# A spectral filter feeding a soft mixture of experts: bank pairs taken in turn, the fold in its own tiles, signs on ScalarE

## The chip, the cores and the metric

The kernel runs on one core of one Trainium2 chip. The core has five engines with instruction queues of their own: TensorE (PE in the profile; its weight loads are listed as PEld), VectorE (DVE), ScalarE (ACT), GpSimd (POOL) and SyncE (SP), which here issues nearly all transfers. Sixteen DMA engines carry the transfers between HBM and the on-chip memory SBUF. TensorE writes its results to PSUM, which has eight banks of 2 KB per partition. The metric is the device time of one execution in microseconds; a time of a kernel is the median of its runs.

## What is computed

```
x: (8, 2496, 256)   filt_r, filt_i: (1249, 256)   phi: (256, 32)   w1: (8, 256, 1024)   w2: (8, 1024, 256)

X = rfft(x, axis=1);  Y = X * (filt_r + i filt_i);  y = irfft(Y, n=2496, axis=1)     # global filter
x = y.reshape(19968, 256)
logits = x @ phi                                    # 32 slots, 4 for each of 8 experts
d = softmax of logits over the 19968 tokens
slot_input = d.T @ x
slot_out[e] = relu(slot_input[e] @ w1[e]) @ w2[e]   # for each expert e
c = softmax of logits over the 32 slots
out = c @ slot_out
```

Everything is float32. The transform of length 2496 is split as 39 x 64. It is a real transform, so half of the spectrum is enough.

## The kernel before

**Stages.** The forward transform of a batch has two stages. The first (length 39, over six units of a batch, `PIECE`, L53) starts from data that is *folded*: sums and differences of mirrored tokens. `load_x` (L345) brings a unit's tokens into a tile xt, `fold_x` (L358) makes the sums and differences in four elementwise operations, `s1_unit` (L380) does four pairs of matmuls into two PSUM banks, and ScalarE copies the result to a tile called at (L407). `store_a` (L413) writes it to a scratch tensor in HBM, a_dram, and `load_ash` (L438) reads it back with the other index ahead. `x_pair` (L474) is the second stage (length 64): eight matmuls into two PSUM banks, then on VectorE the complex product with the filter, which is two multiplications (L510, L512) and two sums (L513, L514). For batches 6 and 7 the sums run on GpSimd and the second multiplication writes to SBUF. `t_pair` (L516) turns the result, ScalarE copies it, and `l_unit` (L531) multiplies by phi, still in the frequency domain. From the logits of a group of batches a long chain of small steps (`chain`, L576) makes the softmax over tokens and adds to the slots' inputs; it is cut into pieces at its `yield`s, and `hop` puts a piece or two into each slot. Batch 0 takes another way into its first stage (`first_stage`, `turn`) that needs no fold and no trip through HBM. After the last batch come the experts and the output (from L1071).

**Slots.** The main loop (L937) runs over slots n = 0 to 81, ten to a batch. Each even slot below 80 has one x_pair, so 40 pairs in all; t_pair follows one pair later, l_unit in the odd slot behind it. `slot_of` (L81) gives each of the 42 first-stage units of batches 1 to 7 its slot: batch 1's units lie in slots 0 to 4, one in each, later batches have six units in ten slots, one in each even slot and one more in an odd one. Slot 64 (`last_s1`) has the last. From there x has the only bank pair of its own, and the other one goes to the chain.

**What sets the order.** Each engine works its queue in order. The program text is not the order by itself: a planner places each engine's instructions by priorities and by its own estimate of when inputs are ready. `behind` (L330) chains instructions of one queue strictly, `not_before` (L354) says that an instruction may not be placed ahead of another one; it is a lower bound, with no wait on the chip. All transfers of L337 on SP are chained in the order of the program text. TensorE's order within a pair is given by such bounds through `held`: x (even slot), the first-stage unit of that slot, t of the pair before, then in the odd slot l and the other unit. The fold's operations have bounds only for the first two units.

**Tiles and banks around the change.** PSUM's eight banks: two for x (`ps_x`), two for the first stage (`ps_s1`), two for t and l (`ps_t`), two for the chain (`ps_c`). So x of one pair needs the banks that VectorE still reads for the pair before. Of xt there are `XB` = 6 tiles, of at `AB` = 4, and one (`EB` = 1) for the fold's intermediate sums and differences, called eo. The fold's first two operations read xt and write eo, the last two read eo and write back into xt. So an xt tile comes free when the unit's matmuls are done. The second of the four operations runs on VectorE (`FD = (1,)`), the others on GpSimd; the first two units (`early`) run on VectorE alone. Six loads are issued ahead of the loop, and each `store_a` of a unit issues one more (`next_x`). `sign_tables` (L812) multiplies the imaginary filter table of each of ten columns by a sign, the first two on VectorE, eight on GpSimd.

Of the kernel before, what the change touches and what calls it, by code (L numbers as in the profile page):

```python
# [40 lines left out]
P = 128  # L41
# [4 lines left out]

CPB = NT // 2
PPB = CPB // 2
XB = 6
EB = 1  # L50
FD = (1,)
AB = 4
PIECE = ((0, 1), (1, 3), (3, 5), (5, 7), (7, 9), (9, 11))  # L53
NU = len(PIECE)
NK = N2 // 4
# [227 lines left out]
def fft_soft_moe(ctx, tc, x0, w0, x, ff, phi, wx, cst, w1q, out):  # L283
# [65 lines left out]
        xts[b, c] = t  # L349

    eos = {}
    held = [None] * 6

    def not_before(ins, other):  # L354
# [3 lines left out]
    def fold_x(b, u):  # L358

        lo, hi = PIECE[u]  # L360
        w = (hi - lo) * P
        xs = xts.pop((b, u)).rearrange("q k a d -> q (k a d)")[:, 0 : 4 * w].rearrange("q (k a d) -> q k a d", k=2, a=2)
        eo = proda.tile([P, 2, 2, DIM], F32, tag="eo", name=f"eo{b}_{u}", bufs=EB)
        sd = eo.rearrange("q f a d -> q (f a d)")[:, 0 : 4 * w].rearrange("q (f a d) -> q f a d", f=2, a=2)
        early = (b, u) < (1, 2)
        for k, (o, i0, i1, op) in enumerate((
            (sd[:, 0], xs[:, 0], xs[:, 1], ALU.add),
            (sd[:, 1], xs[:, 0], xs[:, 1], ALU.subtract),
            (xs[:, 0], sd[:, :, 0], sd[:, :, 1], ALU.add),
            (xs[:, 1], sd[:, ::-1, 0], sd[:, ::-1, 1], ALU.subtract),  # L370
        )):
            eng = dve if early or k in FD else pool_e
            ins = eng.tensor_tensor(out=o, in0=i0, in1=i1, op=op)  # L373
            if early:
                not_before(ins, held[4])
        eos[b, u] = xs

    a_dram = {}

    def s1_unit(b, u, floor=None):  # L380
        if u == 0:
            a_dram[b] = scr.tile([P, NT, DIM], F32, tag="a_dram", name=f"a_dram{b}")
        lo, hi = PIECE[u]
        w = (hi - lo) * P
        eo = eos.pop((b, u))
        both = ps_s1[0].tile([P, 2, 2, DIM], F32, tag="s1", name=f"s1_{b}_{u}")
        bf = both.rearrange("q r f d -> q r (f d)")[:, :, 0 : 2 * w]
        with tc.high_priority():
            for c, r in ((1, 0), (1, 1), (0, 0), (0, 1)):
                q = slice(64 * r, 64 * r + 64)  # L390
                ins = pe.matmul(  # L391
                    bf[64 * c : 64 * c + 64, r],
                    w1q_t[q, c],
                    eo[q, c].rearrange("q f d -> q (f d)"),
                    start=True,
                    stop=True,
                )
                held[1] = ins
                if floor is None:
                    behind("pe", ins)  # L400
                else:
                    not_before(ins, floor)
                    if held[2] is not None:
                        not_before(ins, held[2])
        at = proda.tile([P, 4 * DIM], F32, tag="at", name=f"at{b}_{u}", bufs=AB)
        av = at[:, 0 : 4 * w].rearrange("q (f r d) -> q f r d", f=2, r=2)
        copied[0] = act.copy(av, bf.rearrange("q r (f d) -> q f r d", f=2))  # L407
        stores.append((b, u, at))
# [4 lines left out]
    def store_a():  # L413

        while stores:
            b, u, at = stores.pop(0)
            ad = a_dram[b].rearrange("(f r c m) t d -> f r c m t d", f=2, r=2, c=2)
            for c in range(2):
                if u:
                    m = PK * (u - 1)  # L420
                    dst = a_dram[b].rearrange("(g c m) t d -> c g m t d", g=4, c=2)[c, :, m : m + PK]
                    issue(
                        dst.rearrange("g m t d -> (m t) g d"),
                        at[64 * c : 64 * c + PK * HR].rearrange("q (g d) -> q g d", g=4),
                    )
                    continue
                for r in range(2):
                    dst = ad[:, r, c, NJ] if r else ad[c, r, :, NJ]
                    p0 = 64 * c + HR * r
                    issue(dst.rearrange("f t d -> t f d"), at[p0 : p0 + HR, 0 : 2 * DIM].rearrange("q (f d) -> q f d", f=2))  # L430
            next_x()

    ys = {}
    lts = {}
# [39 lines left out]
    def x_pair(b, i):  # L474

        ash = ashs.pop((b, i)).rearrange("q (c k) d -> q c k d", k=2)
        ps = ps_x.tile([P, 2, 2, DIM], F32, tag="x", name=f"x_{b}_{i}")
        first = []
        for r, k in ((0, 0), (0, 1), (1, 0), (1, 1)):
            for lo, hi in ((0, 1), (1, 2)) if i + k == 0 else ((0, 2),):  # L480
# [30 lines left out]
        add, part = (pool_e, y) if b >= PA else (dve, ps)  # L511
        dve.tensor_tensor(out=part, in0=ps, in1=frv, op=ALU.mult)  # L512
        add.tensor_tensor(out=y[:, 1], in0=part[:, 1], in1=t2[:, 1], op=ALU.add)  # L513
        add.tensor_tensor(out=y[:, 0], in0=part[:, 0], in1=t2[:, 0], op=ALU.subtract)  # L514

    def t_pair(b, i):  # L516

# [294 lines left out]
    def sign_tables(c):  # L812
        if c < CPB:
            fi = ff_t[:, c, 1]
            eng = dve if c < 2 else pool_e
            eng.tensor_scalar(out=fi, in0=fi, scalar1=C("sgn", c, c + 1), scalar2=None, op0=ALU.mult)

    NS = BATCH * CPB
    units = [(b, u) for b in range(1, BATCH) for u in range(NU)]
# [6 lines left out]
    def next_x():  # L826
        if xnext:
            load_x(*xnext.pop(0))

    def split_next(n):  # L830
        for b, u in at_slot.get(n, ()):
            fold_x(b, u)

    w0_t = ypool.tile([P, 1024], F32, tag="y", name="w0_t")
# [24 lines left out]
    def load_to(n):  # L859
        while loads:  # L860
            b, i = loads[0]
            if n < max(b * CPB + 2 * i - (3 if b < 2 else 2 * NA - 1), slot_of(b, NU - 1) + (2 if b < 3 else 3)):
                break
            load_ash(*loads.pop(0))

# [8 lines left out]
    s1_unit(1, 0)  # L874
    sign_tables(0)
    sign_tables(1)
    split_next(0)
    last = {bs[-1]: g for g, bs in enumerate(GROUPS)}
    active = []
    late_pool = []  # L880
# [56 lines left out]
    for n in range(NS + LT):  # L937
        if n < NS:
            load_to(n)
            if n == CPB // 2:  # L940
                issue(cst_t[:, NEAR:FAR], cst[:, NEAR:FAR])
            if n == NS - 2 * CPB:
                behind("sp", sp.dma_start(cst_t[:, FAR:], cst[:, FAR:]))
            split_next(n + 1)
            store_a()
        if n % 2 == 0 and n < NS:
            x_pair(*divmod(n // 2, PPB))
        if n < NS:
            sign_tables(n + 2)
            if n + 2 < CPB:  # L950
                turn(n + 2)
        if n % 2 == 0:
            for b, u in at_slot.get(n, ()):
                s1_unit(b, u, held[0])
        if n % 2 == 0 and n >= LT:
            t_pair(*divmod(n // 2 - 1, PPB))
        if n == last_s1:
            store_a()
            proda_cm.__exit__(None, None, None)
            ps_s1_cm.__exit__(None, None, None)  # L960
            ps_s1[0] = ctx.enter_context(tc.tile_pool(name="ps_s2", bufs=2, space=PSUM))
            late_cm, lp = open_pool("late", WL, "right")
            work2_cm, lp2 = open_pool("work2", 1, "left")
            late_pool.extend((lp, lp2))
            wl = iter(range(WL))
# [15 lines left out]
        floor[0] = (held[2] if n % 2 else held[5]) if n > last_s1 else None  # L981
        hop_slot(n)
        floor[0] = None
        if n % 2:
            for b, u in at_slot.get(n, ()):
                s1_unit(b, u, held[2] or held[0])
        if n == FREE:
            load_ws(ypool, "y", (YB - 3 * CPB + NS % YB - CPB) // 2, 2)
            big[0] = ypool.tile([P, PPB, 2, 2, DIM], F32, tag="yb", name="yb_last", bufs=1)
# [208 lines left out]
```

## Time and profile before

| | |
|---|---|
| median of 3 runs | 433.5 us (433.19 to 433.61) |
| the profiled execution | 434.7 us |
| its span, first to last instruction | 432.8 us |
| mean granted TensorE clock | 0.908 |
| TensorE matmul, VectorE, ScalarE, GpSimd busy | 82%, 63%, 40%, 48% of the span |
| SP's transfer queue | 71.4% of 16 DMA engines |

All times of the trace are microseconds from the span's start. An instruction's idle time is that of its engine just ahead of it, and the releaser named with it is what ended that idle time: "DVE eo L373 <- DMA xt<-in_x" means that VectorE stood still ahead of an instruction of line 373 that writes eo, until a transfer into xt had landed. In that notation `out<-in` names the tile written and the tiles read, with numbers left out. A busy TensorE is not one at its peak, since its matmuls overlap and their ends are modelled. The share of DMA is the mean over the 16 engines.

### The profile page before, as it was taken

What the parts mean: (1) busy time and instruction counts of PE and PEld (TensorE: products, weight loads), DVE (VectorE), ACT (ScalarE), POOL (GpSimd) and SP (SyncE); (2) the same over time, 40 slices, a digit from 0 to 9 for tenths busy, and PEclk for the clock granted to TensorE, in tenths of its full rate; (3) what the DMA queues carried; (4) which work ended last, traced back from release to release, by engine and by line L of the source; (5) the groups of instructions that cost most, each with busy time, mean ns of one, the idle gap of its engine ahead of it and who ended that gap; (6) DMA issues with size and microseconds to landing.
All of it is one profiled execution on the core that took longest, in us unless ns stands there. A gap on an engine that the chain in (4) does not pass through costs nothing.

```text
span 432.8 us, 10012 instructions
## 1 busy us (share of the span) xinstructions
PE 352.8 (82%) x4054; PEld 211.2 (49%) x4054; DVE 274.1 (63%) x423; ACT 172.5 (40%) x354; POOL 208.8 (48%) x200
## 2 busy tenths in 40 slices
PE   8959485786795869688779798998998999999970
PEld 7623132333442545344336454555655763687860
DVE  2761566666566958767677888467756645288640
ACT  3443133423335435243255344545423643186530
POOL 0499999686445745456664640444224130363000
PEclk9998799968999698998898899999999999999655
DMA  8995848786748564876776568676469579189997
GB/s 315 399 299 170 272 143 249 226 247 227 232 137 274 154 195 116 242 233 199 247 215 181 153 175 248 179 243 217 123 218 334 229 253 322 38 347 411 418 416 304
DMA packets 42013, 103.88 MB, mean 240 GB/s; under 512 B 4252, under 2 KB 22556, under 8 KB 39792
## 3 DMA queue, kind: packets, MB, share of 16 engines
q1 hardware_dynamic: 41278, 102.89, 71.4%
q8 instruction: 32, 0.52, 0.5%
q10 hardware_dynamic: 690, 0.36, 0.3%
q14 instruction: 13, 0.11, 0.1%
HBM read 63.11 MB, written 40.12 MB: 239 GB/s over the span
## 4 chain that ended last, share of the span: by engine, by line
PE 32%; DMA 20%; DVE 19%; POOL 12%; issue 5%; ACT 5%; SPq 2%; ACTq 0%; DVEq 0%; POOLq 0%
DMA xt<-in_x 14%; POOL xt L373 7%; PE x L485 5%; PE s L391 4%; DVE t L510 3%; DVE x L512 3%; PE out L1148 3%; DMA out<-ob 3%; POOL eo L373 3%; PE v L574 2%; ACT at L407 2%; SPq L337 2%; PE dd L574 2%; DMA phi_t<-in_phi 2%; PE s L574 2%
## 5 line engine op out<-in xcount | busy, mean ns | idle before, releaser
L373 POOL TENSOR_TENSOR xt<-eo 128x512 f32<-128x512 f32 (+1 forms) x80 | 93.6, 1191 | 11.1 <-DVE eo L373 3.2
L373 POOL TENSOR_TENSOR eo<-xt 128x512 f32<-128x512 f32 (+1 forms) x40 | 62.9, 1571 | 65.7 <-DMA xt<-in_x 64.4
L485 PE MATMUL x<-ash,cst_t 64*64 64x512 f32 (+3 forms) x352 | 58.7, 656 | 32.8 <-DVE y L514 18.2
L407 ACT COPY at<-s 128x1024 f32<-128x1024 f32 (+1 forms) x42 | 39.6, 942 | 108.4 <-PE s L391 97.6
L510 DVE TENSOR_TENSOR t<-x,ff_t 128x1024 f32<-128x1024 f32 x40 | 48.9, 1221 | 33.0 <-PE x L485 21.1
L373 DVE TENSOR_TENSOR eo<-xt 128x512 f32<-128x512 f32 (+1 forms) x44 | 29.0, 663 | 60.0 <-DMA xt<-in_x 38.5
L391 PE MATMUL s<-xt,w1q_t 64*64 64x512 f32 (+1 forms) x336 | 49.9, 666 | 5.0 <-POOL xt L373 5.0
L529 ACT COPY yt<-t 128x512 f32<-128x512 f32 x80 | 43.5, 594 | 17.6 <-PE t L523 17.4
L540 PE MATMUL l<-yt,phi_t 128*32 128x128 f32 x640 | 37.3, 286 | 9.1 <-ACT yt L529 7.3
L523 PEld LDWEIGHTS t<-cst_t,y 128*128 128x128 f32 x232 | 26.6, 147 | 25.4 <-issue 18.1
L485 PEld LDWEIGHTS x<-ash,cst_t 64*64 64x64 f32 (+1 forms) x352 | 14.3, 145 | 48.6 <-DVE y L514 21.9
L1148 PE MATMUL out<-so,st 32*128 32x256 f32 x468 | 35.5, 337 | 2.0 <-ACT ob L1153 1.0
L512 DVE TENSOR_TENSOR x<-x,ff_t 128x1024 f32<-128x1024 f32 x30 | 36.8, 1227 | 0.5
L513 POOL TENSOR_TENSOR y<-y,t 128x512 f32<-128x512 f32 x9 | 11.5, 1274 | 48.5 <-DVE y L512 44.4
L523 PE MATMUL t<-cst_t,y 128*128 128x128 f32 x232 | 34.5, 289 | 0.2
L1148 PEld LDWEIGHTS out<-so,st 32*128 32x128 f32 x468 | 30.9, 222 | 5.9 <-ACT ob L1153 3.1
L540 PEld LDWEIGHTS l<-yt,phi_t 128*32 128x32 f32 x640 | 19.2, 110 | 23.8 <-ACT yt L529 21.6
L1153 DVE COPY ob<-out 128x512 f32<-128x512 f32 (+1 forms) x40 | 25.0, 670 | 8.6 <-DMA out<-ob 5.5
L1153 ACT COPY ob<-out 128x512 f32<-128x512 f32 (+1 forms) x40 | 21.8, 581 | 14.9 <-PE out L1148 6.9
L391 PEld LDWEIGHTS s<-xt,w1q_t 64*64 64x64 f32 x336 | 14.5, 154 | 24.6 <-issue 16.3
L551 ACT COPY lt<-l 128x128 f32<-128x128 f32 x40 | 10.7, 269 | 33.1 <-PE l L540 33.1
L574 PE MATMUL s<-y,dd 128*32 128x256 f32 x232 | 18.4, 381 | 0.0
(124 smaller groups left out, 534.5 us busy)
## 6 DMA issues: line engine op xcount, KB each, us to landing
xt<-in_x SPq DMA_DIRECT2D x35, 512.0 KB
ash<-a_dram SPq DMA_DIRECT2D x35, 512.0 KB
out<-ob SPq DMA_DIRECT2D x17, 1024.0 KB
a_dram<-at SPq DMA_DIRECT2D x70, 240.0 KB
w<-in_wx SPq DMA_DIRECT2D x22, 512.0 KB
x_t<-in_x SPq DMA_DIRECT2D x5, 512.0 KB
ff_t<-in_ff SPq DMA_DIRECT2D x10, 256.0 KB
ff_t<-in_wx SPq DMA_DIRECT2D x5, 512.0 KB
```

Source lines behind the costliest of these rows:

```text
L373: ins = eng.tensor_tensor(out=o, in0=i0, in1=i1, op=op)
L391: ins = pe.matmul(bf[64 * c : 64 * c + 64, r], w1q_t[q, c], eo[q, c].rearrange("q f d -> q (f d)"), start=True, stop=True,)
L407: copied[0] = act.copy(av, bf.rearrange("q r (f d) -> q f r d", f=2))
L485: ins = pe.matmul(ps[64 * k : 64 * k + 64, r, lo:hi], w[rows], ash[rows, lo:hi, k], start=True, stop=True)
L510: dve.tensor_tensor(out=t2, in0=ps[:, ::-1], in1=fiv, op=ALU.mult)
L512: dve.tensor_tensor(out=part, in0=ps, in1=frv, op=ALU.mult)
L523: ins = pe.transpose(pt[:, dh, r, :], ys[b, 2 * i + c][:, r, dh * P : (dh + 1) * P], ident)
L529: act.copy(yt[:, c], pt)
L540: ins = pe.matmul(pl[32 * j : 32 * j + 32], phi_t[:, dh, :], yt[:, j // 2, dh, :, N2 * (j % 2) : N2 * (j % 2) + N2], start=(dh == 0), stop ...
L574: line(pe.matmul(*a, **k))
L1148: nc.tensor.matmul(prs[k][:, mm, :], sts[n][q, hs, c0 : c0 + P], so[q, ho], start=(i == 0), stop=(i == 2))
L1153: copy(ob[:, nm * k : nm * (k + 1), :], prs[k])
```

## The change

1. Second transform and first stage share two bank pairs. `x_pair` takes them in turn; `s1_unit` takes the pair that the latest x_pair did not take. When the first stage has ended (`proda_open`), x keeps to one pair as before.
2. The fold writes its sums and differences to a tile sd (`DB` = 2) and its result to a tile eo (`EB` = 2), no longer back into xt. There are five xt tiles instead of six and three at tiles instead of four. For batch 1 the first two operations both run on VectorE.
3. The fold is called three slots ahead of its unit instead of one, behind the slot's x_pair instead of ahead of it. Its VectorE operations may not be placed ahead of the latest pair's last sum (`added`).
4. The next load of xt is issued ahead of each fold instead of behind each store.
5. First-stage units come behind t_pair in even slots, and ahead of l_unit in odd ones, with the latest t or x as their bound.
6. The ash loads of batch 1 may come one slot sooner.
7. All ten signs are done by ScalarE, as a copy with a scale for each partition.

```diff
-XB = 6
-EB = 1
+XB = 5
+EB = 2
+DB = 2
 FD = (1,)
-AB = 4
+AB = 3
...
+    added = [None]
...
         xs = xts.pop((b, u)).rearrange("q k a d -> q (k a d)")[:, 0 : 4 * w].rearrange("q (k a d) -> q k a d", k=2, a=2)
-        eo = proda.tile([P, 2, 2, DIM], F32, tag="eo", name=f"eo{b}_{u}", bufs=EB)
-        sd = eo.rearrange("q f a d -> q (f a d)")[:, 0 : 4 * w].rearrange("q (f a d) -> q f a d", f=2, a=2)
+        sd = proda.tile([P, 4 * DIM], F32, tag="sd", name=f"sd{b}_{u}", bufs=DB)
+        eo = proda.tile([P, 4 * DIM], F32, tag="eo", name=f"eo{b}_{u}", bufs=EB)
+        sd, eo = (
+            t[:, 0 : 4 * w].rearrange("q (f a d) -> q f a d", f=2, a=2) for t in (sd, eo)
+        )
         early = (b, u) < (1, 2)
         for k, (o, i0, i1, op) in enumerate((
             (sd[:, 0], xs[:, 0], xs[:, 1], ALU.add),
             (sd[:, 1], xs[:, 0], xs[:, 1], ALU.subtract),
-            (xs[:, 0], sd[:, :, 0], sd[:, :, 1], ALU.add),
-            (xs[:, 1], sd[:, ::-1, 0], sd[:, ::-1, 1], ALU.subtract),
+            (eo[:, 0], sd[:, :, 0], sd[:, :, 1], ALU.add),
+            (eo[:, 1], sd[:, ::-1, 0], sd[:, ::-1, 1], ALU.subtract),
         )):
-            eng = dve if early or k in FD else pool_e
+            eng = dve if early or k in FD or (b == 1 and k < 2) else pool_e
             ins = eng.tensor_tensor(out=o, in0=i0, in1=i1, op=op)
             if early:
                 not_before(ins, held[4])
-        eos[b, u] = xs
+            elif eng is dve and added[0] is not None:
+                not_before(ins, added[0])
+        eos[b, u] = eo
...
+    turn_of = [1]
+
+    def pair_banks(k):
+        return (ps_s1[0], "s1") if k and proda_open[0] else (ps_x, "x")
+
+    proda_open = [True]
...
-        both = ps_s1[0].tile([P, 2, 2, DIM], F32, tag="s1", name=f"s1_{b}_{u}")
+        pool, tag = pair_banks(1 - turn_of[0])
+        both = pool.tile([P, 2, 2, DIM], F32, tag=tag, name=f"s1_{b}_{u}")
...
-            next_x()
...
-        ps = ps_x.tile([P, 2, 2, DIM], F32, tag="x", name=f"x_{b}_{i}")
+        turn_of[0] = 1 - turn_of[0]
+        pool, tag = pair_banks(turn_of[0])
+        ps = pool.tile([P, 2, 2, DIM], F32, tag=tag, name=f"x_{b}_{i}")
...
-        add.tensor_tensor(out=y[:, 0], in0=part[:, 0], in1=t2[:, 0], op=ALU.subtract)
+        added[0] = add.tensor_tensor(out=y[:, 0], in0=part[:, 0], in1=t2[:, 0], op=ALU.subtract)
...
-            eng = dve if c < 2 else pool_e
-            eng.tensor_scalar(out=fi, in0=fi, scalar1=C("sgn", c, c + 1), scalar2=None, op0=ALU.mult)
+            act.activation(fi, fi, AF.Copy, scale=C("sgn", c, c + 1))
...
         for b, u in at_slot.get(n, ()):
+            next_x()
             fold_x(b, u)
...
-            if n < max(b * CPB + 2 * i - (3 if b < 2 else 2 * NA - 1), slot_of(b, NU - 1) + (2 if b < 3 else 3)):
+            if n < max(b * CPB + 2 * i - (4 if b < 2 else 2 * NA - 1), slot_of(b, NU - 1) + (2 if b < 3 else 3)):
...
-    split_next(0)
+    for n in range(3):
+        split_next(n)
...
-            split_next(n + 1)
             store_a()
         if n % 2 == 0 and n < NS:
             x_pair(*divmod(n // 2, PPB))
         if n < NS:
+            split_next(n + 3)
             sign_tables(n + 2)
...
-        if n % 2 == 0:
-            for b, u in at_slot.get(n, ()):
-                s1_unit(b, u, held[0])
         if n % 2 == 0 and n >= LT:
             t_pair(*divmod(n // 2 - 1, PPB))
+        for b, u in at_slot.get(n, ()):
+            s1_unit(b, u, held[5])
         if n == last_s1:
             store_a()
             proda_cm.__exit__(None, None, None)
+            proda_open[0] = False
...
-        if n % 2:
-            for b, u in at_slot.get(n, ()):
-                s1_unit(b, u, held[2] or held[0])
```

## The prediction

> **What bounds the kernel now.** I read the totals first, then the span cut into four stretches, then the waits of the stretches that have the first stage in them, and last the instructions around one wait.
>
> ```profile
> span 432.8 us, 10012 instructions
> PE 352.8 (82%) x4054; PEld 211.2 (49%) x4054; DVE 274.1 (63%) x423; ACT 172.5 (40%) x354; POOL 208.8 (48%) x200
> ```
>
> No engine is full. The busy time by stretch (columns: busy us and instructions of each engine, granted clock, share of the 16 DMA engines, GB/s):
>
> ```profile
> core 0: us, PE busy (x) PEld busy (x) DVE busy (x) ACT busy (x) POOL busy (x), PEclk, DMA share, GB/s
> 18.00:80.00 62.00, 42.14 (x320) 18.68 (x319) 36.03 (x46) 21.65 (x36) 59.68 (x49) 0.92 0.73 231
> 80.00:262.00 182.00, 146.21 (x1600) 78.63 (x1600) 130.22 (x174) 70.41 (x133) 103.16 (x80) 0.89 0.69 206
> 262.00:331.00 69.00, 64.13 (x810) 37.88 (x810) 45.39 (x62) 29.50 (x61) 22.52 (x18) 1.00 0.66 214
> 331.00:433.00 102.00, 84.37 (x1211) 62.75 (x1211) 54.62 (x125) 43.75 (x107) 21.84 (x50) 0.86 0.79 303
> ```
>
> The change acts in the first two rows: before 18 us there is only loading and batch 0's start, after 262 nothing is folded any more. In the first, GpSimd is full (59.68 of 62). In the second, 182 us long, VectorE works 130.22 and stands 51.8. The waits of these two stretches (total us, times, longest), first 18 to 80, then 80 to 262:
>
> ```profile
> DVE eo L373 <- POOL xt L373: 20.6, 12, 3.7
> ```
> ```profile
> POOL eo L373 <- DMA xt<-in_x: 64.4, 21, 5.6
> DVE eo L373 <- DMA xt<-in_x: 38.5, 16, 5.4
> PE x L485 <- DVE yb L514: 12.0, 5, 3.2
> DVE t L510 <- PE x L485: 10.6, 9, 2.1
> PE x L485 <- DVE y L514: 9.6, 5, 3.6
> ```
>
> Of VectorE's 51.8 idle us, 38.5 stand ahead of one instruction, the second op of the fold (L373), and what it waits for is the load of xt. One such place:
>
> ```profile
> 78.86 0.71 SPq L337 DMA_DIRECT2D xt<-in_x  x1
> 81.79 1.23 DVE L510 TENSOR_TENSOR t<-x,ff_t 128x1024 f32<-128x1024 f32 x1 [1.21 <-PE x L485]
> 85.04 0.69 DVE L373 TENSOR_TENSOR eo<-xt 128x512 f32<-128x512 f32 x1 [2.02 <-DMA xt<-in_x]
> 85.65 1.23 DVE L512 TENSOR_TENSOR x<-x,ff_t 128x1024 f32<-128x1024 f32 x1
> 86.91 0.69 DVE L513 TENSOR_TENSOR yb<-x,t 128x512 f32<-128x512 f32 x1
> 87.51 0.68 DVE L514 TENSOR_TENSOR yb<-x,t 128x512 f32<-128x512 f32 x1
> 88.25 1.98 PE L485 MATMUL x<-ash,cst_t 64*64 64x512 f32 x8 [2.33 <-DVE yb L514]
> 90.56 1.99 PE L391 MATMUL s<-xt,w1q_t 64*64 64x512 f32 x8
> ```
>
> The fold has been put between the two multiplications of a pair. Its load was issued at 78.86 and is there 6 us later; meanwhile L512, whose input has long been ready, stands behind it, then the two sums, and then TensorE, because the one pair of PSUM banks for x is free only after the second sum (2.33 us). And the fold is not urgent at all: the load is issued when an xt buffer comes free, so the fold runs as soon as its data lands, with six buffers up to five units before the first stage wants it. A wait for a distant transfer has been queued ahead of near work.
>
> **The second transform in two bank pairs.** x of pair p+1 no longer waits for the sums of pair p, but for the ScalarE copy of the first stage that last used the other two banks; the first stage of pair p waits for the sums of pair p-1. Warm, the PE pieces of one pair are:
>
> ```profile
> 110.77 1.09 PE L485 MATMUL x<-ash,cst_t 64*64 64x512 f32 x8
> 111.68 1.04 PE L391 MATMUL s<-xt,w1q_t 64*64 64x512 f32 x8
> 112.65 1.09 PE L523 MATMUL t<-cst_t,y 128*128 128x128 f32 x8
> 114.75 0.72 PE L540 MATMUL l<-yt,phi_t 128*32 128x128 f32 x16
> ```
> ```profile
> L373 POOL TENSOR_TENSOR xt<-eo 128x512 f32<-128x512 f32 (+1 forms) x54 | 63.3, 1193 | 10.2 <-DVE eo L373 3.2 <-PE t L523 2.9 <-DVE al L748 2.4
> L373 POOL TENSOR_TENSOR eo<-xt 128x512 f32<-128x512 f32 (+1 forms) x26 | 40.6, 1562 | 64.8 <-DMA xt<-in_x 64.4
> L512 DVE TENSOR_TENSOR x<-x,ff_t 128x1024 f32<-128x1024 f32 x22 | 27.0, 1226 | 0.2
> L510 DVE TENSOR_TENSOR t<-x,ff_t 128x1024 f32<-128x1024 f32 x22 | 26.8, 1220 | 10.8 <-PE x L485 10.6
> L407 ACT COPY at<-s 128x1024 f32<-128x1024 f32 (+1 forms) x27 | 25.2, 934 | 68.8 <-PE s L391 65.7 <-DMA xt<-in_x 3.2
> L373 DVE TENSOR_TENSOR eo<-xt 128x512 f32<-128x512 f32 (+1 forms) x26 | 17.4, 668 | 39.2 <-DMA xt<-in_x 38.5 <-POOL xt L373 0.6
> ```
>
> These groups are of 80 to 262: 22 pairs and 27 first-stage units, so a pair takes 182/22 = 8.27 us, with 130.22/22 = 5.92 of VectorE work. The new loop goes from the sums of p-1 through t (1.09), s (1.04), the copy (0.93), x (1.09) and VectorE's four ops (1.22 + 1.23 + 0.69 + 0.68 = 3.82) to the sums of p+1: 7.97 us for two pairs, 4.0 for one. That lies below 5.92, so the banks themselves bind nothing; s standing after t costs nothing for the same reason. The waits of x for the sums (12.0 + 9.6) and of VectorE for x (10.6) can go.
>
> **The fold.** Three ops for GpSimd and one for VectorE stay, in tiles of their own; VectorE's op now comes behind the second sum of the pair before. An xt buffer is freed by the first two ops instead of by the first stage, and its next load is issued four units ahead: at 27/22 units per pair, more than three pairs, or 18 us at 5.92, against the 6 us that a load took. So the 38.5 us go. On SP the load has moved behind the store of the unit before and ahead of later stores and loads of ash. It waits for the fold of the unit before, which ends about 0.7 us behind the sums; the store ahead of it waits for t, s and the copy, 3 us behind them. So it holds nothing up. At the start three loads now stand ahead of batch 1's first store, behind the first folds; that store is wanted only by pair 5, for which the ash loads also come one slot sooner. What is late next if I am wrong on this: the ash load behind it, and x. After VectorE's op, GpSimd needs 2 x 1.19 us; the first stage comes one whole VectorE pair later, at least 3.82 us. With two sd and two eo tiles GpSimd's earlier op has its tile. Three at buffers instead of four: each has two further units, over 9 us, to be stored. I cost these at nothing; cover gone, each is in the fourth rival below.
>
> **GpSimd and the signs.** In the stretch 18 to 80 VectorE's fold waits 20.6 us for GpSimd, which has one tile for sums and differences and does the signs in between.
>
> ```profile
> L816 POOL TENSOR_SCALAR ff_t<-ff_t,cst_t 128x256 f32<-128x256 f32 x8 | 8.0, 1002 | 16.6 <-DMA ff_t<-in_ff 16.6
> L709 ACT COPY u<-u 128x240 f32<-128x240 f32 x12 | 3.8, 368 | 1.1 <-PE u L574 1.1
> ```
>
> GpSimd loses 8.0 us of signs and four first ops of batch 1 (4 x 1.56 = 6.2): 59.7 - 14.2 = 45.5. VectorE gains 4 x 0.67 = 2.7. ScalarE's ten signs have no row before; nearest is its copy of 128x240, 0.37 us, and the copy of a whole unit, 0.93, bounds it above; nothing of it is a gain on ScalarE, so 3.7 to 9.3 us on an engine with 62 - 21.65 = 40 idle. I take 0.4 each, at no cost to the end. The transfers' floor there is 0.73 x 62 = 45.3. The fullest that this trace keeps any engine over a long stretch is TensorE after 262: 64.13/69 = 0.93. So this stretch should take 45.5/0.93 = 49 us: **minus 13**. Bounds: 45 (minus 17), and 58 (minus 4) if only the signs and a quarter of the waits go.
>
> **The steady stretch.** Floors: VectorE 130.2; TensorE 146.21 x 0.89 = 130.1 at full clock; transfers 0.69 x 182 = 125.6; GpSimd 103.2. Three of them stand level, so what goes from VectorE's waits cannot go on for ever. Take away the 38.5 alone and leave the other 13.3 us of idle as they are, as a stand-in for new small waits: 143.5. Then there is a cost that the old order avoided. These rows show VectorE and GpSimd in each other's way, the same work with company (first and last row) and without:
>
> ```profile
> 143.49 3.69 DVE L680 TENSOR_TENSOR d<-lg,m_run 117x512 f32<-117x512 f32 x3
> 296.33 2.00 DVE L680 TENSOR_TENSOR d<-lg,m_run 117x512 f32<-117x512 f32 x3
> ```
> ```profile
> 120.09 1.27 POOL L373 TENSOR_TENSOR eo<-xt 128x512 f32<-128x512 f32 x1 [2.25 <-DMA xt<-in_x]
> 128.65 1.78 POOL L373 TENSOR_TENSOR eo<-xt 128x512 f32<-128x512 f32 x1 [4.05 <-DMA xt<-in_x]
> ```
>
> So far the load's landing released both engines together, and VectorE's 0.69 us op got in first. From now on it starts when the sums end, with GpSimd perhaps inside an op of 1.2 us. At a GpSimd share of 103.2/150 = 0.69 and half an op lost, 27 x 0.69 x 0.6 = 11 us; in a regular rhythm GpSimd would have finished (2.4 + 1.6 us of a pair's 5.9) when VectorE comes, so I take half, 6: **150 us, minus 32**. Bounds: 130.2/0.93 = 140 (minus 42), and 143.5 + 27 x 0.9 = 168 (minus 14), a wait of most of an op at each fold.
>
> The Trainium skill ("SBUF — State Buffer", Who interferes with whom) speaks against this edit here: a VectorE instruction with two SBUF inputs and a GpSimd instruction that reads SBUF share one port pair, and whichever starts first blocks the other for its whole length. The 3.69 us beside 2.00, and 1.78 beside 1.27, agree. By the rule alone each fold may lose up to a GpSimd op, which is the upper bound above and the third rival; by the rows of the regular rhythm it loses little.
>
> **The rest.** After 262 the work is the same, with x in one bank pair again. Only the last folds, done early before, now meet GpSimd's sums:
>
> ```profile
> 253.68 1.79 POOL L373 TENSOR_TENSOR eo<-xt 128x512 f32<-128x512 f32 x1 [3.94 <-DMA xt<-in_x]
> 271.36 1.27 POOL L513 TENSOR_TENSOR y<-y,t 128x512 f32<-128x512 f32 x1 [13.28 <-DVE y L512]
> ```
>
> One fold, 1.56 + 2 x 1.19 = 3.9 us, may stand among them: 0 to plus 4; I take **plus 1**, since GpSimd idles before most of them.
>
> **Sum.** -13 - 32 + 1 = -44. The profiled execution took 434.7 us, its span of 432.8 and 1.9 around it; so its like becomes 390.7, with a span of 389. The median of the runs is 433.5, 1.2 lower: **389.5 us**.
>
> **Rivals.**
> 1. TensorE becomes the bound at its present clock. For it: clock 0.89 and 146.2 busy us in the stretch; 146.2/0.93 = 157. The first stretch then gives about 10 instead of 13: 433.5 - 25 - 10 + 1 = 399.5. Against it: the slow pieces (1.98 and 1.99 above, against 1.09 and 1.04) stand behind idle time that would shrink, and after 262 the clock is 1.00. By the Trainium skill ("TensorE: Matmul & The Clock Gate", Part 1) the clock halves after an idle window of some 3.4 us and comes back with work. The trace agrees at 88.25, and by that rule the clock would rise and the 157 fall to 140.
> 2. Every wait goes: 140 and 45 us, no loss behind: 433.5 - 42 - 17 = 374.5. For it: the loop of 4.0 us leaves room. Against it: three floors of equal height.
> 3. VectorE is blocked at each fold: 168 us, and half of the first gain, 6: 433.5 - 14 - 6 + 1 = 414.5. For it are the L680 rows, against it the rhythm.
> 4. Slower: folds come late and hold TensorE. They no longer run five units ahead, and the order given to them is a floor, not a place; a planner may put VectorE's op behind the next pair's sums as well. Then s waits at the head of TensorE's queue, with t done, and l, the routing chain and x behind it. The loop for two pairs: fold 0.69, a blocked 1.27, GpSimd 1.27 + 2.4, s 1.99 and x 1.98 at the slow clock, copy 0.93, four VectorE ops 3.82, and the pair's remaining TensorE work, (146.2/22 - 1.98 - 1.99 - 1.09) x 2 = 3.2: 17.6, or 8.8 a pair. It decides from 2 x 8.27 = 16.5 on. 22 x 0.53 = 12 us more, nothing won before: 433.5 + 12 = 445.5. Against it: it needs the late place, the port and the slow clock at once; with the warm pieces it stays below 16.5.
> 5. The change does not do what it says: the fold's place in VectorE's queue changes, but VectorE still meets unlanded loads, since SP issues them late. Nothing but the signs is won: about 433. Against it stand the four units of lead.
>
> **Chances.** Forecast 0.56, rival 1 0.20, rival 2 0.08, rival 3 0.08, rival 4 0.05, rival 5 0.03. The range 371 to 418 leaves out rivals 4 and 5 and the ends of 2 and of the forecast. A difference of 0.2%, about 0.9 us, is what a measurement of this kernel can tell from none: faster 0.92, same 0.03, slower 0.05.
>
> **What would show it.** In the profile after: VectorE's wait for DMA at the fold near 0 instead of 38.5, and for GpSimd far below 20.6; x of the next pair issued while VectorE is still on the last one; a pair near 6.8 us (150/22); the clock in the steady stretch above 0.89; GpSimd free of signs. The fold's mean on VectorE shows the port: 0.67 if free, 1.3 or more if rival 3 holds. TensorE waiting for GpSimd at L391 in the steady stretch would be rival 4, a TensorE over 95% busy at a clock of 0.89 rival 1. I am wrong if the fold's wait for DMA stays above 15 us, or if it goes and the span moves by less than 20.

## The result, and the profile after

The changed kernel takes 381.8 us (median of 4 runs, 380.88 to 384.09) against 433.5 us; the ratio is 0.882, with a 95% interval of 0.878 to 0.886. That is 51.7 us less, and the prediction said 44 (389.5 us). The profiled execution took 384.1 us, the longest of the four. Medians here are of all runs of a kernel; ratios and intervals leave out a run more than 1.5% above the fastest of its kernel.

First the totals of the kernel after:

```profile
span 382.3 us, 10013 instructions
PE 336.3 (88%) x4054; PEld 204.9 (54%) x4054; DVE 282.2 (74%) x425; ACT 178.3 (47%) x364; POOL 188.4 (49%) x188
```

VectorE's busy time grew from 274.1 to 282.2 us, while the span lost 50.5. The time came out of idle time. To see where, both traces are cut at the same pairs: the starts of the first product (the op that writes t from x) of the pairs numbered 0, 7, 30 and 39. Busy time by stretch, the columns as in the prediction, first the kernel before:

```profile
19.96:81.79 61.83, 41.34 (x321) 18.35 (x325) 35.00 (x44) 21.07 (x35) 59.92 (x48) 0.92 0.72 226
81.79:268.86 187.07, 150.56 (x1651) 81.18 (x1647) 134.79 (x179) 72.94 (x138) 101.40 (x78) 0.89 0.69 207
268.86:329.15 60.29, 56.82 (x741) 33.55 (x733) 38.40 (x52) 25.90 (x54) 22.52 (x18) 1.00 0.64 207
329.15:432.80 103.65, 86.17 (x1225) 64.00 (x1225) 56.47 (x126) 44.82 (x109) 21.84 (x50) 0.86 0.79 305
```

and the kernel after, at the same pairs:

```profile
core 0: us, PE busy (x) PEld busy (x) DVE busy (x) ACT busy (x) POOL busy (x), PEclk, DMA share, GB/s
21.62:63.50 41.88, 35.01 (x317) 15.86 (x313) 36.95 (x43) 22.49 (x40) 33.51 (x29) 1.00 0.93 303
63.50:216.83 153.33, 138.30 (x1646) 73.81 (x1645) 138.39 (x181) 74.11 (x138) 103.03 (x84) 0.97 0.78 256
216.83:277.57 60.74, 56.61 (x738) 33.44 (x736) 39.76 (x54) 26.14 (x54) 27.88 (x22) 0.97 0.66 210
277.57:382.30 104.73, 87.78 (x1225) 66.76 (x1225) 56.78 (x126) 45.31 (x109) 21.79 (x50) 0.83 0.80 301
```

| stretch | before | after | difference |
|---|---|---|---|
| up to pair 0 | 19.96 | 21.62 | +1.7 |
| pairs 0 to 7 | 61.83 | 41.88 | -20.0 |
| pairs 7 to 30 | 187.07 | 153.33 | -33.7 |
| pairs 30 to 39 | 60.29 | 60.74 | +0.4 |
| from pair 39 to the end | 103.65 | 104.73 | +1.1 |

From pair 7 to pair 30, VectorE was busy for 134.79 of 187.07 us and is now busy for 138.39 of 153.33: a pair has 6.02 us of its work (138.39/23) and 0.65 of its idle time, where it had 5.86 and 2.27. The first stretch now has GpSimd at 33.51 of 41.88 us and the transfers at 0.93, so there the transfers are what is nearest to full.

The waits of the kernel after, from 18 to 262 us (total us, times, longest). A window in microseconds holds more pairs of a faster kernel, so waits of two kernels are compared here only where the difference is large. The two waits of the fold on VectorE, and TensorE's wait with x for the sums, which led the lists of before, have no row any more. Three rows of what is left on TensorE and VectorE matter for the argument (the others are of 6.0 us at most, the largest of them in the routing chain, ahead of l and behind GpSimd's sums):

```profile
DVE t L526 <- PE x L501: 8.2, 11, 1.7
PE x L501 <- ACT at L422: 6.4, 17, 0.6
PE s L406 <- POOL eo L378: 1.9, 1, 1.9
```

The groups of the fold's first two ops, GpSimd's and VectorE's in the same window and then VectorE's between the pairs 7 and 30, show no idle time ahead of VectorE's (the last number):

```profile
L378 POOL TENSOR_TENSOR sd<-xt 128x512 f32<-128x512 f32 (+1 forms) x36 | 43.2, 1203 | 2.4
L378 DVE TENSOR_TENSOR sd<-xt 128x512 f32<-128x512 f32 (+1 forms) x44 | 34.8, 813 | 0.0
...
L378 DVE TENSOR_TENSOR sd<-xt 128x512 f32<-128x512 f32 (+1 forms) x28 | 20.4, 740 | 0.0
```

And in order of time, two places of the kernel after:

```profile
87.09 0.68 DVE L530 TENSOR_TENSOR y<-x,t 128x512 f32<-128x512 f32 x1
87.69 1.02 DVE L378 TENSOR_TENSOR sd<-xt 128x256 f32<-128x256 f32 x2
88.08 1.09 PE L501 MATMUL x<-ash,cst_t 64*64 64x512 f32 x8
89.23 1.23 DVE L526 TENSOR_TENSOR t<-x,ff_t 128x1024 f32<-128x1024 f32 x1 [0.53 <-PE x L501]
...
129.07 1.09 PE L501 MATMUL x<-ash,cst_t 64*64 64x512 f32 x8
...
134.21 0.68 DVE L530 TENSOR_TENSOR y<-x,t 128x512 f32<-128x512 f32 x1
```

At 87.69 the fold starts right behind the second sum of the pair, with its data there, and x runs beside it. At 129.07 TensorE makes the next x five microseconds before the pair in hand has its last sum (134.21): this is the second bank pair at work.

### The profile page after: what moved, and what is told of

Its sections match the earlier page's. It is cut to its first block, busy times and chain, and to the rows that moved or that the text cites. A ratio compares the mean times of both kernels' runs of the same rounds, so it can differ in the third digit from the quotient of the medians.

```text
span 382.3 us, 10013 instructions
## 1 busy us (share of the span) xinstructions
PE 336.3 (88%) x4054; PEld 204.9 (54%) x4054; DVE 282.2 (74%) x425; ACT 178.3 (47%) x364; POOL 188.4 (49%) x188
## 4 chain that ended last, share of the span: by engine, by line
PE 51%; DVE 18%; DMA 12%; ACT 7%; issue 4%; POOL 3%; SPq 1%; DVEq 0%; ACTq 0%; POOLq 0%
PE x L501 8%; PE t L539 7%; PE s L406 6%; DMA xt<-in_x 5%; PE out L1162 5%; ACT at L422 4%; PE u L590 4%; DVE t L526 3%; PE v L590 3%; PE dd L590 3%; PE l L556 2%; DMA out<-ob 2%; PE s L590 2%; DMA ff_t<-in_ff 2%; DVE d L696 2%
## 5 line engine op out<-in xcount | busy, mean ns | idle before, releaser
L378 POOL TENSOR_TENSOR eo<-sd 128x512 f32<-128x512 f32 (+1 forms) x80 | 100.7, 1280 | 75.7 <-DVE sd L378 50.4
L501 PE MATMUL x<-ash,cst_t 64*64 64x512 f32 (+3 forms) x352 | 50.8, 594 | 8.6 <-ACT at L422 6.4
L406 PE MATMUL s<-eo,w1q_t 64*64 64x512 f32 (+1 forms) x336 | 42.8, 578 | 5.7 <-ACT at L422 3.7
L378 POOL TENSOR_TENSOR sd<-xt 128x512 f32<-128x512 f32 (+1 forms) x36 | 43.2, 1203 | 2.4
L539 PEld LDWEIGHTS t<-cst_t,y 128*128 128x128 f32 x232 | 25.6, 143 | 21.2 <-DVE y L530 6.2
L378 DVE TENSOR_TENSOR sd<-xt 128x512 f32<-128x512 f32 (+1 forms) x48 | 36.8, 791 | 0.0
L556 PE MATMUL l<-yt,phi_t 128*32 128x128 f32 x640 | 29.8, 285 | 5.9 <-ACT yt L545 5.7
L1162 PEld LDWEIGHTS out<-so,st 32*128 32x128 f32 x468 | 32.8, 253 | 3.4 <-DVE ob L1167 1.4
L556 PEld LDWEIGHTS l<-yt,phi_t 128*32 128x32 f32 x640 | 16.6, 110 | 19.4 <-ACT yt L545 12.5
L590 PEld LDWEIGHTS u<-cst_t,d 117*64 117x64 f32 (+3 forms) x440 | 16.0, 141 | 5.4 <-issue 2.9
L590 PE MATMUL u<-cst_t,d 117*64 117x60 f32 (+3 forms) x440 | 18.1, 237 | 0.8 <-issue 0.8
```

What stands on the lines that cost most here:

```text
L406: ins = pe.matmul(bf[64 * c : 64 * c + 64, r], w1q_t[q, c], eo[q, c].rearrange("q f d -> q (f d)"), start=True, stop=True,)
L501: ins = pe.matmul(ps[64 * k : 64 * k + 64, r, lo:hi], w[rows], ash[rows, lo:hi, k], start=True, stop=True)
L539: ins = pe.transpose(pt[:, dh, r, :], ys[b, 2 * i + c][:, r, dh * P : (dh + 1) * P], ident)
L556: ins = pe.matmul(pl[32 * j : 32 * j + 32], phi_t[:, dh, :], yt[:, j // 2, dh, :, N2 * (j % 2) : N2 * (j % 2) + N2], start=(dh == 0), stop ...
L590: line(pe.matmul(*a, **k))
L1162: nc.tensor.matmul(prs[k][:, mm, :], sts[n][q, hs, c0 : c0 + P], so[q, ho], start=(i == 0), stop=(i == 2))
```

## The experiments

The theory was that the gain is the end of VectorE's wait for unlanded loads, and that the other edits only cover what would then be late. Its rivals: that the banks or the signs carry the gain; that the position given to the fold matters little once it has tiles and lead of its own; and that the fold in its new place still costs through the port that VectorE and GpSimd share. Medians are given with the ratio to the kernel before, run beside them (434.8, 433.4 and 435.0 us for the three groups of runs), and its 95% interval.

### One part alone, added to the kernel before

**The order alone.** Tiles, lead, loads, banks and signs stay as before.

```diff
+    added = [None]
...
                 not_before(ins, held[4])
+            elif eng is dve and added[0] is not None:
+                not_before(ins, added[0])
...
-        add.tensor_tensor(out=y[:, 0], in0=part[:, 0], in1=t2[:, 0], op=ALU.subtract)
+        added[0] = add.tensor_tensor(out=y[:, 0], in0=part[:, 0], in1=t2[:, 0], op=ALU.subtract)
```

> The kernel before with one edit: VectorE's fold operation may not be placed ahead of the latest pair's last sum. Tiles, banks, loads and signs stay as before. If the bound alone frees VectorE, its wait for xt (38.5 us between 80 and 262) falls below 10 and the time to about 405. If the bound is too loose, because the load is issued as late as before and the fold still stands directly behind it, the wait stays above 25 and the time within 6 us of 433.5.

Measured: 406.9 us (0.940, 0.933 to 0.948). Its waits from 18 to 262 us:

```profile
DVE t L513 <- PE x L488: 31.8, 22, 3.6
PE s L394 <- POOL xt L374: 22.3, 19, 4.2
DVE eo L374 <- POOL xt L374: 17.4, 7, 3.7
```

The wait for the load is gone by this bound on the order alone, and with it about 26 us. But the fold is then just one slot ahead of its unit, so TensorE waits for GpSimd (22.3 us), and VectorE for x behind it.

**The bank pairs in turn alone.** Only part 1 of the change, on the kernel before.

```diff
-        both = ps_s1[0].tile(...)
+        pool, tag = pair_banks(1 - turn_of[0])
+        both = pool.tile(...)
...
-        ps = ps_x.tile(...)
+        turn_of[0] = 1 - turn_of[0]
+        pool, tag = pair_banks(turn_of[0])
+        ps = pool.tile(...)
```

> The kernel before with one edit: x and the first stage take two bank pairs in turn. Fold, loads, order and signs stay as before. If the fold's place was the cause, VectorE still stands behind unlanded loads and the time is 424 to 434. If x waiting for its banks was the cause (waits of 12.0 + 9.6 us on TensorE and 10.6 us on VectorE), the time is 405 or less.

Measured: 427.8 us (0.986, 0.980 to 0.992). The waits of the fold from 18 to 262 us are as they were (38.5 and 21.2 before):

```profile
DVE eo L373 <- DMA xt<-in_x: 37.1, 21, 4.8
DVE eo L373 <- POOL xt L373: 23.0, 10, 3.7
```

The banks give some 6 us while the fold stands in the way. They do not carry the gain of 52.

### One part undone in the kernel after

**Fixed bank pairs.** x and the first stage keep a pair each.

```diff
-        pool, tag = pair_banks(1 - turn_of[0])
+        pool, tag = ps_s1[0], "s1"
...
-        pool, tag = pair_banks(turn_of[0])
+        pool, tag = ps_x, "x"
```

> The changed kernel with x and the first stage each on a bank pair of its own, as before the change; all else of the change stays. If the fold carries the gain, 387 to 397. If the banks carry it, 410 or more. Either way TensorE's wait of x for the sums comes back.

Measured: 385.3 us (0.886, 0.878 to 0.894), less than even the first expectation. The interval overlaps that of the kernel after: at most a few of the 52 us hang on the banks here. A second pair of kernels follows below.

**No order for the fold.** The tiles, the three slots of lead and the early loads stay; VectorE's fold may be placed anywhere again.

```diff
-            elif eng is dve and added[0] is not None:
-                not_before(ins, added[0])
```

> The changed kernel without the bound that keeps VectorE's fold operation behind the latest sum; tiles, four units of load lead, banks and signs stay. If the bound is what keeps VectorE free, folds go ahead of near work again and the time is 392 or more. If the lead of the loads and the two tiles each for sums and results are enough, the time is within 3 us of 381.8.

Measured: 386.7 us (0.893, 0.887 to 0.898), between the two expectations. The groups of the fold from 18 to 262 us, in this kernel:

```profile
L378 POOL TENSOR_TENSOR sd<-xt 128x512 f32<-128x512 f32 (+1 forms) x36 | 47.7, 1330 | 2.2
L378 DVE TENSOR_TENSOR sd<-xt 128x512 f32<-128x512 f32 (+1 forms) x44 | 45.1, 1036 | 9.7 <-POOL eo L378 9.6
```

So the order and the lead are two cures for the same wait. With the lead, loads have landed wherever the fold stands, and no wait of VectorE for DMA has a row even without the order. What the order still does is to keep the two engines apart: without it the same 44 ops take 45.1 us instead of 34.8, GpSimd's 36 take 1.33 us each instead of 1.20, and VectorE waits another 9.6 us for GpSimd. Of these 20 us of VectorE's time, 5 reach the end.

**Signs back on VectorE and GpSimd.**

```diff
-            act.activation(fi, fi, AF.Copy, scale=C("sgn", c, c + 1))
+            eng = dve if c < 2 else pool_e
+            eng.tensor_scalar(out=fi, in0=fi, scalar1=C("sgn", c, c + 1), scalar2=None, op0=ALU.mult)
```

> The changed kernel with the signs where they were: two on VectorE, eight on GpSimd. It asks how much of the first 18 us (from the products of pair 0 to those of pair 7) came from freeing GpSimd. If GpSimd's load set that stretch, as the prediction had it, 8 us more: about 390. If the fold's two tiles and its place did, GpSimd has room and the time stays within 3 us of 381.8.

Measured: 385.1 us (0.887, 0.881 to 0.894), 3.3 us above the kernel after and nearer to the second expectation; the two intervals overlap. Its stretch from pair 7 to pair 30:

```profile
69.14:219.24 150.10, 134.97 (x1647) 72.06 (x1646) 138.13 (x181) 74.18 (x138) 103.21 (x84) 0.99 0.79 262
```

Pair 7 comes at 69.14 instead of 63.50, and the next 23 pairs take 150.1 us instead of 153.3. So the signs moved to ScalarE are 5.6 us of the gain of the first stretch. The 3 us behind it are no loss that is shown: the profiled execution of the kernel after lies 2.3 us above its median and this one 0.9 below, and the code of those pairs is the same. What the signs are worth at the end cannot be told from nothing here.

**Less lead.** The fold, and the load issued with it, one slot ahead of the unit (where the fold was before the change), and in a second kernel two slots (the same with `range(2)` and `n + 2`); the change has three.

```diff
-    for n in range(3):
-        split_next(n)
+    split_next(0)
...
-            split_next(n + 3)
+            split_next(n + 1)
```

> The changed kernel with the fold, and the load issued with it, called one slot ahead of the unit instead of three; the bound behind the latest sum stays and is that of a later pair. If the two slots of lead hide GpSimd's part of the fold, TensorE now waits for GpSimd at the first stage (over 20 us in total) and the time is 395 to 410: the prediction's fourth rival in a milder form. If the planner places the folds early anyway, it stays within 4 us of 381.8.

> The kernel after with the fold and its load two slots ahead of the unit instead of three (one slot ahead gave 418.9). My estimate gave the three-slot lead one whole VectorE pair, at least 3.8 us, to spare. If that cover is right, one slot less (about half a pair, 3.3 us) still nearly covers GpSimd's 2.4 us: 382 to 388. If the load's time is what the lead must cover, half of the loss comes back: about 400.

Measured: 418.9 us with one slot (0.965, 0.959 to 0.971) and 390.0 us with two (0.900, 0.893 to 0.908). The waits from 18 to 262 us, with one slot:

```profile
DVE t L526 <- PE x L501: 46.8, 20, 8.0
PE s L406 <- POOL eo L378: 34.2, 21, 6.2
```

and with two:

```profile
DVE t L526 <- PE x L501: 22.5, 22, 2.7
PE s L406 <- POOL eo L378: 15.0, 16, 1.5
```

The first stage waits for the fold, and VectorE for the x that stands behind it in TensorE's queue: 34.2, 15.0 and 1.9 us for one, two and three slots. The first slot of added lead is worth 29 us and the second 8. One slot ahead came out dearer than expected, and slower than the order alone (406.9), which also folds one slot ahead. Of these 12 us, 10.9 are there by pair 7 (84.99 against 74.05), where batch 1 has a unit in each slot, and 1.9 come between the pairs 7 and 30 (165.97 against 164.06). A difference that could account for it is that for a unit in an odd slot the fold there stands ahead of the slot's x_pair and here behind it; this was not tried, and the tiles and the place of the loads differ too. The kernel with one slot from pair 7 to pair 30, and one of its waits in order of time:

```profile
84.99:250.96 165.97, 139.21 (x1648) 73.33 (x1648) 136.90 (x182) 74.80 (x138) 101.82 (x85) 0.97 0.77 238
```
```profile
102.46 1.09 PE L406 MATMUL s<-eo,w1q_t 64*64 64x512 f32 x8 [1.41 <-POOL eo L378]
```

Between these pairs TensorE waits 17.5 of the 34.2 us at a clock of 0.97, and the first stage behind the wait takes 1.09 us, where the prediction's slow piece took 1.99. With two slots the wait is short at each place (1.5 us at the longest), as the cover of one VectorE pair less half a pair would have it, and the time lies just above the end of that expectation. Tiles, the place of the loads, batch 1's first op on VectorE, the place of the first stage and the earlier ash loads were not undone one by one.

### Is VectorE what binds now?

Four kernels take work off VectorE in the kernel after: the fold's second op to GpSimd, for all units or for the even ones (batch 1 stays), and the copies v and u2 of the chain's first three groups to ScalarE. For half of the fold, the condition `k in FD` becomes `(k in FD and u % 2)` instead of the first edit.

```diff
-FD = (1,)
+FD = ()
...
-            dve.tensor_copy(v[:, s0 : s0 + n, :], pv[:, 0:n])
+            (dve.tensor_copy if late else act.copy)(v[:, s0 : s0 + n, :], pv[:, 0:n])
...
-            ended[1] = dve.tensor_copy(u2[...], pu[:, 0:n]...)
+            ended[1] = (dve.tensor_copy if late else act.copy)(u2[...], pu[:, 0:n]...)
```

The fold on GpSimd:

> The changed kernel with the fold's second operation on GpSimd too (all but batch 1's first two operations). VectorE loses some 35 x 0.7 = 24 us of work, GpSimd gains 35 x 1.2 = 42. If VectorE is the bound of the steady stretch (138.4 of 153.3 us busy), the time falls to 365 to 375. If GpSimd's five microseconds a unit become the bound, or TensorE is (138.3 of 153.3), it stays at 380 or rises to 395.

The copies on ScalarE:

> The changed kernel with the routing chain's copies out of PSUM at the lines of v and u2 moved from VectorE to ScalarE for the first three groups: some 10 us off VectorE. If VectorE is the bound, 374 to 378. If VectorE and TensorE hold each other level, within 2 us of 381.8.

Both together:

> The kernel after with two loads taken off VectorE: the fold's second op goes to GpSimd (batch 1's first two ops stay on VectorE), and the routing chain's copies v and u2 of the first three groups go to ScalarE. Alone they gave 374.5 and 377.2. If VectorE is still what binds with the fold gone from it, the gains add: about 370. If GpSimd binds then (124.9 of 136 us busy in the run with the fold on GpSimd alone), the copies give nothing: 374.5, within 1.5.

The copies and half of the fold:

> As the run with both moves, but the fold's second op goes to GpSimd only for the even units of a batch, so that VectorE and GpSimd share it. If each of the two engines binds when it has the whole of it, this is the fastest: about 371. If the gain of the fold on GpSimd came from VectorE's order being free of folds, and not from busy time, half of the folds keep half of the loss: about 376.

| kernel | median us | ratio | 95% interval |
|---|---|---|---|
| after | 381.8 | 0.882 | 0.878 to 0.886 |
| copies on ScalarE | 377.2 | 0.868 | 0.863 to 0.874 |
| fold on GpSimd | 374.5 | 0.863 | 0.858 to 0.868 |
| both | 373.7 | 0.863 | 0.856 to 0.870 |
| copies and half of the fold | 374.2 | 0.863 | 0.856 to 0.870 |

Either load taken off VectorE makes the kernel faster, so VectorE's time does bind in the kernel after. But the gains do not add, and half of the fold came out between its two expectations. From pair 7 to pair 30, one row each of the fold on GpSimd, of both, and of half of the fold:

```profile
63.11:211.06 147.95, 136.99 (x1649) 73.90 (x1649) 125.29 (x153) 74.86 (x138) 137.15 (x115) 0.97 0.81 264
```
```profile
63.46:210.22 146.76, 134.02 (x1649) 72.33 (x1648) 119.38 (x141) 79.99 (x150) 137.30 (x116) 0.99 0.82 268
```
```profile
62.81:209.00 146.19, 133.90 (x1645) 71.19 (x1643) 126.49 (x156) 79.76 (x150) 120.95 (x100) 1.00 0.81 268
```

The expectation put the missing gain down to a full GpSimd (137.30 of 146.76 us, 0.94). The last row speaks against that: GpSimd is relieved to 120.95 (0.83), VectorE has 126.49 (0.87), and the stretch is not shorter by more than 0.6 us. What stands equally high in all three is TensorE: 0.93, 0.91 and 0.92 busy at a clock of 0.97 to 1.00, with the same matmuls. That TensorE is the next limit is only read from these shares: no run took work off TensorE, and VectorE's wait for x in this stretch, 18.7 and 18.9 us in the first two kernels, is 4.4 us in the third.

**Fixed bank pairs, with the copies on ScalarE.** The two edits above together.

> The kernel after with the chain's copies on ScalarE (377.2 with banks in turn), and with the bank pairs fixed as before: x and the first stage each keep their own pair. If the banks bind once VectorE's load is lighter, this loses what the wait of x for the sums costs, 380 or more. If VectorE's busy time decides all the same, within 1.5 of 377.2.

Measured: 381.9 us (0.881, 0.874 to 0.887) against 377.2 (0.868, 0.863 to 0.874) with the banks in turn. In the waits from 18 to 262 us, TensorE meets the sums again:

```profile
DVE t L526 <- PE x L501: 16.6, 19, 3.6
PE x L501 <- DVE y L530: 5.7, 9, 1.1
PE x L501 <- DVE yb L530: 4.1, 7, 1.1
```

The intervals just part: the banks in turn are worth about 5 us here, as they were worth 6 in the kernel before. In the kernel after itself their 3.5 us (385.3 against 381.8) are within the intervals. They are a small part of the 52 us either way.

## Why the prediction was right, and where it was not

**What bounds the kernel** held. The 38.5 us of VectorE's wait for xt are gone, and the bound on the order alone, which touches nothing else, brings half of the whole gain. That the transfer was late and the fold not urgent is shown twice, by the order alone and by the kernel without the order. It is a wait of the steady stretch; the 20 us of the first stretch have another source, below.

**The banks** were costed as binding nothing by themselves, with the waits of x (12.0 + 9.6) and of VectorE for x (10.6) able to go. The waits of x for the sums are gone, VectorE still waits 4.5 us for x between the pairs 7 and 30, where it waited 11.1, and alone the banks give 6 us.

**The fold's cover** held for the change as it is: no wait of the fold's VectorE op for DMA, 1.9 us of the first stage for GpSimd. The prediction gave the two slots of added lead no price, only a place among the things that are late if the cover goes. The runs price it: 37 us from three slots to one. That is the fourth rival's mechanism, TensorE waiting at the head of its queue for a late fold. Its conditions were too narrow: it let the loss decide only with the port and the slow clock at once, and counted nothing won before. With one slot the clock was low before pair 7 (0.84, with 15.7 us of these waits), but 17.5 us came behind it at 0.97, and the kernel still beat the one before by 14.5 us.

**The steady stretch** was the best-sized term: 150 us for 22 pairs, 6.8 a pair, and -32; measured 6.67 a pair, and -33.7 over 23. The idle time kept as a stand-in, 13.3 us, came out as 14.9 (153.33 - 138.39). The port's loss was put at 6 us: the fold's mean rose from 0.668 to 0.740 us between pairs 7 and 30, which is 28 x 0.072 = 2 us (both means mix two shapes). Its upper bound, 0.9 us at each fold, and the third rival with it, did not come; the kernel without the order comes part of the way, at 1.036 us from 18 to 262 us.

The prediction called this a cost that the old order avoided. It did not avoid it: it put it on GpSimd. These are GpSimd's first ops of the fold between the pairs 7 and 30, before and after (least, middle and longest ns, first and last start):

```profile
L373 POOL TENSOR_TENSOR eo<-xt x26: 966/1776/1804, 85.1 to 253.7; 128x512 f32<-128x512 f32 x22, 128x256 f32<-128x256 f32 x4
L378 POOL TENSOR_TENSOR sd<-xt x28: 725/1272/1608, 64.9 to 214.5; 128x512 f32<-128x512 f32 x24, 128x256 f32<-128x256 f32 x4
```

The mean fell from 1.56 to 1.22 us. With the order alone it is 1.21, and VectorE's op takes 0.640 us there, so the new place by itself lowered both. On GpSimd that is about 10 us of an engine that had been busy for 101.40 of the 187.07 us.

**The first stretch** was the step that failed in size: -13, with bounds of -4 and -17. Between pairs 0 and 7 it is -20.0, and pair 7 comes 18.3 us earlier; both lie outside. The floor of 45.5/0.93 counted all that GpSimd did from 18 to 80 us as work that this stretch needs, less signs and batch 1's four ops. (Nor is 0.93 the fullest that the trace shows: GpSimd's own 59.68 of 62 is 0.96.) But part of it were folds run ahead of their use. With the lead set by slots they are no longer done there: between the same pairs GpSimd has 33.51 us in 29 instructions, where it had 59.92 in 48, 19 fewer and not 12. The same stretch of the kernel with the order alone, and of the one with one slot of lead:

```profile
19.85:74.05 54.20, 41.05 (x321) 18.09 (x325) 32.84 (x41) 21.08 (x35) 42.56 (x37) 0.94 0.82 260
21.96:84.99 63.03, 41.63 (x310) 16.88 (x307) 37.11 (x45) 22.12 (x39) 31.90 (x27) 0.84 0.64 192
```

The order alone brings GpSimd to 42.56 us with the signs still there, below the 45.5 that were counted without them, so 45.5 was no floor. But a free GpSimd is not enough: with one slot of lead it works only 31.90 us, and the stretch is as long as before (63.03 against 61.83), with TensorE waiting 15.7 us for the fold. Two slots give 44.43 and three 41.88. So the gain here hangs on the lead, which the prediction gave no price, and 5.6 us of it on the signs. The second floor, 45.3 us of transfers, had loads ahead in it too: 0.72 x 61.83 = 44.5 us of transfers became 0.93 x 41.88 = 38.9. The transfers now stand highest, and with the fold's op off VectorE the stretch is still 40.36 us, at 0.92; that they end it was not tried by itself.

**The signs** on ScalarE, all ten as one line of the kernel after (least, middle and longest ns, first and last start):

```profile
L831 ACT ACTIVATE ff_t<-ff_t,cst_t x10: 508/509/523, 12.6 to 26.6; 128x256 f32<-128x256 f32 x10
```

They take 0.51 us each, 5.1 in all, inside the bounds; the choice of 0.4 was low. The 1.7 us by which pair 0 comes later (21.62 against 19.96), which the prediction had not counted, is not theirs: with the signs back pair 0 comes at 21.66, and with one slot of lead at 21.96. Its cause stays open.

**The rest** was +1; measured +0.4 and +1.1 in the two last stretches.

**The other rivals.** TensorE as the bound at its old clock fell by the clock: 0.89 rose to 0.97 between pairs 7 and 30, and TensorE is 0.90 busy there. The prediction reads the slow x at 88.25 as agreeing with the rule that it cites; the idle time on that row is 2.33 us, shorter than the window named there, so the row shows slow pieces behind idle time, and not the window's length. "Every wait goes" (374.5) is where the kernels with VectorE relieved arrive, though by less work on VectorE, and not by the loss of its last waits.

## What to carry to other kernels

An engine that works its queue in order is held by the latest input of anything in it, so the first thing to ask of an idle engine is whether the op it stands before is urgent; here a prefetched, distant op cost 38.5 us of waiting, and moving it behind the near work took one bound on the order. Placing such an op later pays in full only with lead bought for it: that bound alone brought 26 us, and in the changed kernel the same fold one slot ahead instead of three cost 37 us of the 52. And a floor made from an engine's busy time in a window counts work that only ran there early, so cut the two traces at the same unit of work before sizing a term.

## What was not expected of the hardware

In these runs the cost of VectorE and GpSimd meeting depended on who came when, more than on how busy they were. With GpSimd busy for 103 of 153 us (0.67) the fold's op on VectorE, which reads two SBUF operands, takes 0.74 us between the pairs 7 and 30; without its place behind the sums, 1.04 us from 18 to 262 us, against 0.81 with it in that same window. With the fold two slots ahead and one slot ahead, the same window gives:

```profile
L378 DVE TENSOR_TENSOR sd<-xt 128x512 f32<-128x512 f32 (+1 forms) x44 | 29.9, 701 | 0.0
```
```profile
L378 DVE TENSOR_TENSOR sd<-xt 128x512 f32<-128x512 f32 (+1 forms) x44 | 31.9, 745 | 0.0
```

The op is cheaper in these two kernels than in the kernel after, though both are slower. By the Trainium skill ("SBUF — State Buffer", Who interferes with whom) the shared port pair is locked for the length of the op that has it; the lengthened ops on both engines without the order (1.04 and 1.33 us) agree. How much of it is met is a matter of the order, and of the 20 us of VectorE's time that the worse order cost, 5 us reached the end.
